# Cosformer attention and an MLP mixer on one core: the first batch in halves of the heads, its u inside the output's products

## Chip, core and metric

The kernel runs on one core of one Trainium2 chip. The metric is device time in microseconds of one execution. TensorE (PE in the profile) does the matrix products and writes PSUM; VectorE (DVE) and ScalarE (ACT) carry results from PSUM to SBUF; GpSimd (POOL) casts in SBUF; SyncE (SP) does nothing but issue transfers. Each engine works its own instructions in the order in which the program writes them, and waits for the others by semaphores. PSUM is handed out in two pools: `ps_mm` with four tiles of one bank, `ps_at` with two tiles of two banks.

## The reference

For each of 8 batches (8 heads, 576 positions, 64 values per head), attention without softmax and then an MLP over positions and one over channels:

```
phi(x) = concat(relu(x) * cos(theta_s), relu(x) * sin(theta_s))      # 64 -> 128 features
kv  = einsum(phi(k), v)            z = sum over s of phi(k)
x   = einsum(phi(q), kv) / (einsum(phi(q), z) + 1e-6)                # (576, 512), heads side by side
u   = x + (relu(x.T @ w_tok1) @ w_tok2).T                            # w_tok1 576x256, w_tok2 256x576
out = u + relu(u @ w_ch1) @ w_ch2                                    # w_ch1 512x1536, w_ch2 1536x512
```

Inputs and output are float32; the products run in bfloat16.

## The kernel before

**Tiles.** The 576 positions are four chunks of 128 (`R` = 4, position 4p + r in partition p of chunk r) and a tail of 64 (`R` again, as the index of the fifth chunk). The tails of two batches share one tile of 128 partitions, the even batch in the lower half, the odd one in the upper. `ORDER` = 0, 1, 2, tail, 3 is the order in which chunks are worked.

**Two halves of a batch.** `Front` is attention and token mixing: features of k and q (`feature`, line 276 on DVE and 274 on ACT), values into `v_aug` (287 on ACT, 289 on DVE or POOL), `kv` (334), q turned to have features in partitions (`q_trans`, 354, and `q_trans_last` for the tail, 366; copied to SBUF by ACT, 358 and 369), `num` (382, then the division on DVE, 390 to 392), `tok1` (405, relu in 410 and 412), `tok2` (429, sum with x on DVE in 432, giving u). `Channel` is the channel MLP: `c_main` (573) makes 12 blocks `mi` of w_ch1's product, each of four matmuls of 512 columns, whose relu ACT writes to `h1T` (577); `o_step` (606) adds two of 12 w_ch2 products to an output chunk; the last adds u (DVE, 611) and stores (615).

**Order.** All order is written out by hand (`manual_schedule`, line 76). The front of batch b + 1 is woven into the channel steps of batch b: `pieces` (483) lists (slot, piece), and the loop from line 784 runs step i and then the pieces of slot i. Batch 0 has nothing to hide behind: `first_front` (667) writes its front out instruction by instruction, with `busy` (210), matmuls on zeros into an unused PSUM tile, where TensorE would wait. It ends with u of batch 0 made directly in transposed form: `turned_x` (448) turns x through an identity product, `turned_b` (455) adds the token mixing, lines 743 and 744 copy to `uT`, and `c_block` (583) makes the first three blocks of the channel product, one quarter of the contraction at a time. Plain u, which the output needs, is made by `tok2` in slots 4 to 10 of batch 0's channel (plan from line 494).

**Batch 0's steps.** Steps 0 to 11 are the 12 blocks of c (the first three are done by then); steps 12 to 23 do output chunks 0 and 1 in thirds of w_ch2 (four products of chunk 0, four of chunk 1, and so on), steps 24 to 35 chunks 2 and 3. `O` = 12 in the plan. Batch 1's kv, turned q, num, tok1 and tok2 lie in slots 11 to 25.

**Loads.** SP issues, in this order: q of batch 0's first four heads, q's tail, k in two halves of the heads, k's tail, v's first half, its tail, v's second half, w_tok1, w_tok2, eight pieces of w_ch1, then batch 1's k, v and q, each with its tail (lines 104 to 137 and 750 to 769). The second half of q is issued by ACT. The weights land as float32 in tiles that are used for other things later. ACT casts w_tok1 (220) and permutes w_tok2 (223, 225); POOL casts w_ch1 (217). The tail rows of w_tok1 come by two casting transfers from POOL (200). w_ch2 comes in three casting transfers from POOL (204), written in slot 8 between POOL's two casts of batch 1's values (289). Batch 2's k and q wait for the second of these three (line 796).

Of the kernel before, what the change touches and what calls it, by code (L numbers as in the profile page):

```python
# [16 lines left out]
def kernel(  # L17
# [76 lines left out]

    def tiles():
        return tuple(io.tile([P, H, R * D], F32, name=n) for n in ("qt", "vt", "kt"))
# [19 lines left out]
    w_tok1n = stage1[:, 0:R * D_tok].rearrange("p (r t) -> p r t", r=R)  # L116
    w_tok2n = stage2[:, 0:NT * S].rearrange("p (n s) -> p n s", n=NT)
    nc.sync.dma_start(out=w_tok1n, in_=moe_w_tok1[0:SM, :].rearrange("(p r) t -> p r t", r=R))
    nc.sync.dma_start(out=w_tok2n, in_=moe_w_tok2.rearrange("(n t) s -> t n s", t=P))
# [77 lines left out]
    nc.gpsimd.memset(tail0.kp[half(1)], 0.0)  # L197
# [21 lines left out]
    def cast_tok1(mi):  # L219
        nc.scalar.copy(w_tok1[:, :, mi * P:(mi + 1) * P], w_tok1n[:, :, mi * P:(mi + 1) * P])  # L220

    def permute_tok2(ki):
        nc.scalar.copy(w_tok2[:, ki, 0:SM].rearrange("t (r p) -> t r p", r=R),
                       w_tok2n[:, ki, 0:SM].rearrange("t (p r) -> t r p", r=R))
        nc.scalar.copy(w_tok2[:, ki, SM:].rearrange("t (g s) -> t g s", g=2),
                       w_tok2n[:, ki, None, SM:S].to_broadcast([P, 2, ST]))


    class Front:
        def __init__(self, b, res, tail):  # L230
# [5 lines left out]

            self.alone = b < 2
            self.kp, self.qp, self.d_sb = {}, {}, {}

            self.qpT = once.tile([P, R * H, P], BF16, name="qpT")  # L240
            self.kv_sb = [twos.tile([P, HH, DP], BF16, name=f"kv_sb{g}") for g in range(2)]
            self.x = once.tile([P, R, Dm], BF16, name="x_sb")
# [16 lines left out]
        def feature(self, which, ci, j, heads=(0, H), on_act=False):  # L259
# [8 lines left out]
            else:  # L268
                t = self.tail
                dst, src = (t.kp, t.kt) if which == "k" else (t.qp, t.qt)  # L270
                rows = self.rows if self.alone else slice(0, P)
                w, o_ap, i_ap = w[rows], dst[rows, lo:hi, j, :], src[rows, lo:hi, :]
            if on_act:
                nc.scalar.activation(o_ap, i_ap, AF.Relu, bias=bias0[0:w.shape[0]], scale=w)
# [16 lines left out]
        def ksum(self, ci, heads=(0, H)):  # L291

            if not hasattr(self, "ks_ps"):
                self.ks_ps = ps_mm.tile([P, H], F32, name="ks_ps", tag="mm")
                self.ks_first = True
# [550 lines left out]
```

## Time and profile before

| what | value |
|---|---|
| median of 3 runs | 269.82 us (269.08 to 270.65) |
| the profiled execution | 270.21 us, span 268.4 us |
| batch 0's front until its first c block product (583) | 0 to 24.33 us |
| first three c blocks | 24.33 to 26.92 us |
| the other nine, and u of batch 0 | 26.92 to 36.87 us |
| batch 1's kv until the outputs take w_ch2's second third | 36.87 to 43.98 us |
| from there to batch 1's first c product | 43.98 to 57.51 us |
| the rest | 57.51 to 268.4 us |

The span is the stretch from the first to the last instruction that the profile shows. In a timeline each line gives start, duration from the first start to the last end, engine, source line, operation, destination and source tiles, shape and count, and in brackets the idle time of the engine before it and what ended that. In the chain of waits each line is a start, a length and what the end of the program hung on then. Weight tiles are named by the buffer they land in: `u_sb` is both w_tok1's and w_tok2's landing place, `w_stage`, `o_stage` and `u_stage` are w_ch1's.

### The profile page before, as it was taken

What the parts mean: (1) busy time and instruction counts of PE and PEld (TensorE: products, weight loads), DVE (VectorE), ACT (ScalarE), POOL (GpSimd) and SP (SyncE); (2) the same over time, 40 slices, a digit from 0 to 9 for tenths busy, and PEclk for the clock granted to TensorE, in tenths of its full rate; (3) what the DMA queues carried; (4) which work ended last, traced back from release to release, by engine and by line L of the source; (5) the groups of instructions that cost most, each with busy time, mean ns of one, the idle gap of its engine ahead of it and who ended that gap; (6) DMA issues with size and microseconds to landing.
All of it is one profiled execution on the core that took longest, in us unless ns stands there. A gap on an engine that the chain in (4) does not pass through costs nothing.

```text
span 268.4 us, 5119 instructions
## 1 busy us (share of the span) xinstructions
PE 259.9 (97%) x2026; PEld 138.9 (52%) x2047; DVE 164.3 (61%) x378; ACT 129.2 (48%) x230; POOL 15.5 (6%) x34
## 2 busy tenths in 40 slices
PE   7989999999999999999999999999999999999994
PEld 2665456455644455446644455446644455445543
DVE  4964598785566846776565846776565846820022
ACT  3955885328606372546606362546516362526400
POOL 5008150010000000000000000000000000000000
PEclk9999999999999999999999999999999999999999
DMA  7999999979999999389954989479974580280032
GB/s 216 316 383 395 327 169 197 330 176 280 196 333 293 265 204 324 114 212 271 228 207 117 286 188 322 120 187 235 242 248 117 156 120 0 59 199 0 2 114 81
DMA packets 92263, 55.25 MB, mean 206 GB/s; under 512 B 59472, under 2 KB 85968, under 8 KB 92240
## 3 DMA queue, kind: packets, MB, share of 16 engines
q1 hardware_dynamic: 89808, 52.24, 72.3%
q0 software_dynamic: 1904, 2.16, 4.5%
q10 hardware_dynamic: 528, 0.52, 0.6%
q8 instruction: 16, 0.26, 0.4%
q14 instruction: 7, 0.06, 0.1%
HBM read 35.85 MB, written 9.44 MB: 169 GB/s over the span
## 4 chain that ended last, share of the span: by engine, by line
PE 78%; DMA 11%; SPq 4%; DVE 4%; issue 1%; POOL 1%
PE o_ps L606 33%; PE c_ps L573 24%; PE u_ps L429 6%; PE b_ps L405 6%; PE ct_ps L593 4%; DMA w_stage<-in_moe_w_ch_dram 4%; DMA vt<-in_v_dram 4%; DMA w_ch<-in_moe_w_ch_dram 3%; PE kv_ps L334 3%; DVE x_sb L392 2%; PE num_ps L382 2%; SPq L86 2%; SPq L92 2%; DVE den L390 1%; DVE den L391 1%
## 5 line engine op out<-in xcount | busy, mean ns | idle before, releaser
L606 PE MATMUL o_ps<-w_ch,h1T 128*128 128x512 bf16 (+1 forms) x380 | 92.6, 372 | 0.9 <-DMA w_ch<-in_moe_w_ch_dram 0.2
L573 PE MATMUL c_ps<-uT,w_ch 128*128 128x512 bf16 (+2 forms) x384 | 91.9, 372 | 0.1
L577 ACT ACTIVATE h1T<-c_ps 128x512 bf16<-128x512 f32 x93 | 55.4, 598 | 59.5 <-PE c_ps L573 59.2
L606 PEld LDWEIGHTS <-h1T 128*128 128x128 bf16 x396 | 37.3, 98 | 40.1 <-issue 0.5
L573 PEld LDWEIGHTS <-w_ch 128*128 128x128 bf16 x384 | 33.5, 97 | 29.9 <-issue 0.2
L611 DVE TENSOR_TENSOR o_sb<-o_ps,u_sb 128x512 f32<-128x512 f32 (+1 forms) x33 | 22.2, 674 | 29.9 <-PE o_ps L606 29.8
L436 ACT CAST u_bf<-u_sb 128x512 bf16<-128x512 f32 x28 | 17.2, 618 | 16.8 <-DVE u_sb L432 13.3
L432 DVE TENSOR_TENSOR u_sb<-u_ps,x_sb 128x512 f32<-128x512 f32 x32 | 21.7, 688 | 5.7 <-PE u_ps L429 5.6
L429 PE MATMUL u_ps<-B,w_tok 128*128 128x512 bf16 x79 | 22.5, 379 | 0.2
L410 ACT ACTIVATE B<-b_ps 128x512 bf16<-128x512 f32 (+1 forms) x9 | 4.8, 549 | 33.7 <-PE b_ps L405 33.7
L392 DVE TENSOR_TENSOR x_sb<-num_ps,den 128x512 bf16<-128x512 f32 x28 | 19.4, 691 | 1.0
L593 PEld LDWEIGHTS <-w_ch 128*128 128x128 bf16 x192 | 13.9, 98 | 8.7
L276 DVE TENSOR_SCALAR kp<-kt,cos_t 128x512 bf16<-128x512 f32 x32 | 15.4, 485 | 4.7 <-DMA kt<-in_k_dram 4.7
L405 PE MATMUL b_ps<-x_sb,w_tok 128*128 128x512 bf16 x63 | 17.7, 379 | 0.1
L593 PE MATMUL ct_ps<-uT_tail,w_ch 128*128 128x128 bf16 x192 | 16.9, 219 | 0.0
L276 DVE TENSOR_SCALAR qp<-qt,cos_t 128x512 bf16<-128x512 f32 (+1 forms) x34 | 15.4, 453 | 1.4 <-DMA qt<-in_q_dram 1.3
L287 ACT CAST v_aug<-vt 128x512 bf16<-128x512 f32 (+1 forms) x28 | 15.6, 594 | 0.1
L276 DVE TENSOR_SCALAR qp<-qt,sin_t 128x512 bf16<-128x512 f32 (+1 forms) x34 | 15.4, 452 | 0.0
L611 DVE TENSOR_TENSOR o_sb<-o_ps,u_tail 128x512 f32<-128x512 f32 x4 | 2.8, 692 | 19.0 <-PE o_ps L606 19.0
L382 PEld LDWEIGHTS <-qpT 128*128 128x128 bf16 x256 | 11.5, 98 | 5.2 <-issue 0.8
L382 PE MATMUL num_ps<-kv_sb,qpT 128*128 128x65 bf16 x256 | 12.9, 193 | 0.5 <-DVE x_sb L392 0.5
L276 DVE TENSOR_SCALAR kp<-kt,sin_t 128x512 bf16<-128x512 f32 x28 | 13.4, 480 | 0.0
(96 smaller groups left out, 225.1 us busy)
## 6 DMA issues: line engine op xcount, KB each, us to landing
out_dram<-o_sb SPq DMA_DIRECT2D x29, 256.0 KB, 2.9
kt<-in_k_dram SPq DMA_DIRECT2D x7, 1024.0 KB, 6.7
vt<-in_v_dram SPq DMA_DIRECT2D x7, 1024.0 KB, 6.8
qt<-in_q_dram SPq DMA_DIRECT2D x7, 1024.0 KB, 8.8
w_stage<-in_moe_w_ch_dram SPq DMA_DIRECT2D x3, 512.0 KB, 10.3
w_ch<-in_moe_w_ch_dram POOLq DMA_DIRECT2D x3, 512.0 KB, 8.6
out_dram<-o_sb SPq DMA_DIRECT2D x10, 128.0 KB, 2.4
qtt<-in_q_dram SPq DMA_DIRECT2D x8, 128.0 KB, 5.5
```

Of the source, the lines that this page charges most:

```text
L276: nc.vector.tensor_scalar(o_ap, i_ap, scalar1=w, scalar2=0.0, op0=ALU.mult, op1=ALU.max)
L382: nc.tensor.matmul(num_ps[:, g, j * DP:j * DP + D1], self.qT_of(ci, h), self.kv_sb[g][:, j, 0:D1], start=True, stop=True)
L392: nc.vector.tensor_mul(self.x_of(ci)[rows].rearrange("p (g j d) -> p g j d", g=2, j=HH), nv[:, :, :, 0:D], den.to_broadcast([rows.stop - r ...
L405: nc.tensor.matmul(self.b1_ps[mi], w, self.x_of(ci), start=(ci == ORDER[0]), stop=(ci == ORDER[-1]))
L429: nc.tensor.matmul(u_ps, w_tok2[:, ki, ci * P:(ci + 1) * P], self.B1[:, ki, :], start=(ki == 0), stop=(ki == NT - 1))
L432: nc.vector.tensor_add(u, u_ps[rows], self.x_of(ci)[rows])
L436: nc.scalar.copy(self.ub[:, ci, :], u)
L573: nc.tensor.matmul(c_ps[:, lo:hi], w_ch1[:, ki, mi * P:(mi + 1) * P], uT[:, lo // P:hi // P, ki, :], start=(ki == 0), stop=(ki == NCC - 1))
L577: nc.scalar.activation(self.h1T[:, mi, :], c_ps, AF.Relu)
L593: nc.tensor.matmul(self.ct_ps[:, mi % R, :], w_ch1[:, ki, mi * P:(mi + 1) * P], self.tail.uT[:, ki, :], start=(mi % R == 0 and ki == 0), s ...
L606: nc.tensor.matmul(o_ps, h, w_ch2[:, ki, cols], start=ki == 0, stop=ki == NCH - 1)
L611: nc.vector.tensor_add(o_sb, o_ps, u)
```

## The change

Batch 0's front works in two halves of four heads each, from k's features to the turned products; token mixing gives half of B's columns per pass. Its kv, kept in `ps_mm`, its sums of k, denominators, products and divisions exist once per half. w_tok1's cast and one half of w_tok2's permutation go from ACT to POOL. The tail rows of w_tok1 come in float32 through SP. Blocks 0 to 2 of c begin when half of the turned blocks are there.

The tail queries of batches 0 and 1 are loaded into the unused half of the tile that takes their tail keys, so that one pair of feature instructions makes both (`load_beside`, `q_trans_beside`).

Batch 0 makes no plain u of its four chunks. `o_mix` starts each output's sum with w_tok2's product, and x is added instead of u at the end. x of batch 0 therefore lives until the outputs are stored, and batch 1's x takes a buffer of the `keep` pool; `B1` gets two buffers.

In the plan for batch 1, k's features, the values and kv come later, and kv, turned q and the first products are put together in slot 13, behind two `o_mix` steps, with four `busy` matmuls. Batch 0 has four more steps.

```diff
+    def load_beside(dst, src, b):
+        return nc.sync.dma_start(out=dst[half(1 - b)],
+                                 in_=src[b, :, SM:S, :].rearrange("h s d -> s h d"))
...
-    load_tail(qtt0, q, 0)
     load_main(kt0, k, 0, 0, HH)
-    load_main(kt0, k, 0, HH, H)
     load_tail(ktt0, k, 0)
+    load_beside(ktt0, q, 0)
     load_main(vt0, v, 0, 0, HH)
     load_tail(vtt0, v, 0)
+    load_main(kt0, k, 0, HH, H)
     load_main(vt0, v, 0, HH, H)
...
     nc.sync.dma_start(out=w_tok1n, in_=moe_w_tok1[0:SM, :].rearrange("(p r) t -> p r t", r=R))
+    for g in range(2):
+        nc.sync.dma_start(out=w_tail1n[half(g), :], in_=moe_w_tok1[SM:S, :])
...
-    for g in range(2):
-        nc.gpsimd.dma_start(out=w_tail1[half(g), :], in_=moe_w_tok1[SM:S, :])
...
+    def cast_tok1(ci):
+        if ci < R:
+            nc.gpsimd.tensor_copy(w_tok1[:, ci, :], w_tok1n[:, ci, :])
+        else:
+            nc.gpsimd.tensor_copy(w_tail1, w_tail1n)
+
+    def permute_tok2(ki, copy):
+        copy(w_tok2[:, ki, 0:SM].rearrange("t (r p) -> t r p", r=R),
+             w_tok2n[:, ki, 0:SM].rearrange("t (p r) -> t r p", r=R))
+        copy(w_tok2[:, ki, SM:].rearrange("t (g s) -> t g s", g=2),
+             w_tok2n[:, ki, None, SM:S].to_broadcast([P, 2, ST]))
...
+        def num_half(self, ci, g):
+            num_ps = ps_at.tile([P, 2, 512], F32, name="num_ps", tag="at")[:, 0, :]
+            for j in range(HH):
+                nc.tensor.matmul(num_ps[:, j * DP:j * DP + D], self.qT_of(ci, g * HH + j),
+                                 self.kv_sb[g][:, j, 0:D], start=True, stop=True)
...
+        def tok1_half(self, ci, g):
+            for mi in range(NT):
+                if ci == ORDER[0]:
+                    self.b1_ps[mi, g] = ps_mm.tile([P, DH], F32, name="b1_ps", tag="mm")
...
+                nc.tensor.matmul(self.b1_ps[mi, g], w, self.x_of(ci)[:, g * DH:(g + 1) * DH],
+                                 start=(ci == ORDER[0]), stop=(ci == ORDER[-1]))
...
+        def q_trans_beside(self):
...
+            qT_ps = ps_mm.tile([P, H, ST], BF16, name="qT_ps", tag="mm")
             for h in range(H):
                 nc.tensor.transpose(qT_ps[:, h, :],
...
+                                    self.tail.kp[rows, h, :, :].rearrange("p a b -> p (a b)"),
+                                    ident[rows, rows])
+            nc.scalar.copy(self.tail.qpT[:, :, half(g)], qT_ps)
...
+                plan = [(6, KS, 0), (6, KS, 1), (8, KS, 2, True), (9, KS, 3, True), (9, KS, R),
+                        (10, before.tok2, R, None, False), (11, V, 0, act), (11, V, 2, pool),
+                        (11, load_w_ch2, 0), (11, V, 3, pool), (11, load_w_ch2, 1),
+                        (11, load_w_ch2, 2), (11, V, R, nc.vector), (11, V, 1, act)]
+                plan += [(O + 1, KV, ci) for ci in range(NSC)]
+                plan += [(O + 1, self.kv_out, (0, 1), (0, 1)), (O + 1, self.q_trans_beside),
+                         (O + 1, QS, 0), (O + 1, fill, 2), (O + 1, QT, 0),
+                         (O + 1, QS, 1), (O + 1, fill, 1), (O + 1, QT, 1),
+                         (O + 1, QS, 2), (O + 1, fill, 1), (O + 1, QT, 2), (O + 1, N, R),
+                         (O + 1, QS, 3, True), (O + 1, N, 0), (O + 2, N, 1), (O + 3, QT, 3),
+                         (O + 5, N, 2), (O + 6, N, 3), (O + 8, before.tail_cast)]
...
-                at, mix, t = (), O + 7, O + 11
+                at, mix, t = (), O + 7, O + 9
...
-            plan += [(mix, self.mix_head, 0), (mix + 1, self.mix_head, 1),
-                     (mix + 2, self.mix_tail)]
...
+            plan += [(mix, self.mix_head, 0), (mix + 1 - first, self.mix_head, 1),
+                     (mix + 2 - first, self.mix_tail)]
...
+        def o_mix(self, ci):
+            self.o_ps[ci] = ps_mm.tile([P, Dm], F32, name="o_ps", tag="mm")
+            for ki in range(NT):
+                nc.tensor.matmul(self.o_ps[ci], w_tok2[:, ki, ci * P:(ci + 1) * P],
+                                 self.res["B1"][:, ki, :], start=(ki == 0), stop=False)
...
     def first_front(f):
...
         for ci in range(R):
...
+            f.feature("k", ci, 0, heads[0])
+            f.feature("k", ci, 1, heads[0])
+            busy(idle_ps, 2)
+            f.ksum(ci, 0)
+            f.values(ci, nc.scalar, heads[0])
         f.k_side(R)
...
+        f.q_trans_beside()
         for ci in range(R):
...
+            f.feature("k", ci, 0, heads[1])
+            if ci < 3:
+                f.feature("k", ci, 1, heads[1])
         for ci in range(NSC):
             f.kv(ci, (0,))
         f.kv_out((0,))
...
+        for ci in range(NSC):
+            cast_tok1(ci)
+        permute_tok2(1, nc.gpsimd.tensor_copy)
         cast_ch1()
...
+        f.kv_out((1,), on_act=(1,))
+        f.num_half(ORDER[4], 0)
+        f.dens(1)
+        f.dens_out(1)
+        permute_tok2(0, nc.scalar.copy)
+        for ci in ORDER[:2]:
+            f.num_half(ci, 1)
+        for ci in ORDER[2:]:
+            f.tok1_half(ci, 0)
+        for mi in range(NT):
+            f.tok1_out_half(mi, 0)
+        for kb in range(2):
+            t_ps[kb] = ps_mm.tile([P, SM], F32, name="t_ps", tag="mm")
+            f.turned_x(t_ps[kb], kb)
+        for i in range(3):
+            f.num_half(ORDER[i + 2], 1)
+            if i < 2:
+                f.tok1_half(ORDER[i], 1)
...
+        for kb in range(2):
+            turned(kb, nc.scalar.copy)
+        for ci in ORDER[2:]:
+            f.tok1_half(ci, 1)
+        for mi in range(NT):
+            f.tok1_out_half(mi, 1, on_act=(mi == 0))
...
+        for mi in range(2):
+            c.c_block(mi, 0)
+        for kb in (2, 3):
+            turned(kb, nc.vector.tensor_copy if kb == 3 else nc.scalar.copy)
...
-            if tails and (b % 2 == 0 or b == 1):
+            if tails and (b % 2 == 0 or b == 1 and n != "q"):
                 load_tail(tail_dst, src, b | 1)
+            if b == 1 and n == "k":
+                load_beside(ktt, q, b)
...
-            if b == 0 and i == NCH:
+            if b == 0 and i == NCH + 2:
                 load_batch(2, "kq", behind=w_ch2_done[1], tails=False)
```

`turned(kb, copy)` is `turned_b` and the copy to `uT`. `tok1_out_half` is the relu of one half on ACT or DVE.

More of the change, by code (lines that the diff above doesn't have):

```diff
@@ L332, in kv @@
+        def kv(self, ci, halves=(0, 1)):
+            if ci == 0 and halves == (0, 1):
+                both = ps_at.tile([P, 2, 512], F32, name="kv_ps", tag="at")
+                self.kv_ps = {g: both[:, g, :] for g in range(2)}
+            elif ci == 0:
+                self.kv_ps[halves[0]] = ps_mm.tile([P, 512], F32, name="kv_ps", tag="mm")
             for g in halves:
@@ L746, in first_front @@
+        for mi in range(2):
+            c.c_block(mi, 1)
+        for kb in range(2):
+            c.c_block(2, kb)
+        for kb in (2, 3):
             for mi in range(AHEAD):
```

259 lines of the change are left out of this document (115 added, 144 removed).

## Prediction

> **What bounds the kernel now.** I read the page first, then the stretches, then the chain of waits in order of time, then the timelines of ScalarE and SP. The page:
>
> ```profile
> span 268.4 us, 5119 instructions
> PE 259.9 (97%) x2026; PEld 138.9 (52%) x2047; DVE 164.3 (61%) x378; ACT 129.2 (48%) x230; POOL 15.5 (6%) x34
> ```
>
> TensorE is busy nearly throughout, so time is won only by fewer matmuls or by waits that end earlier. The stretches (us, then busy time and count of each engine, granted clock, DMA share, GB/s) show where waits are left:
>
> ```profile
> 24.33:26.92 2.59, 2.59 (x13) 1.18 (x12) 0.72 (x2) 0.54 (x2) 2.17 (x5) 1.00 1.08 382
> 26.92:36.87 9.95, 9.90 (x46) 4.50 (x46) 6.78 (x14) 8.30 (x16) 4.35 (x7) 1.00 1.00 279
> 36.87:43.98 7.11, 6.37 (x112) 4.76 (x112) 6.13 (x16) 5.70 (x9) 0.17 (x1) 1.00 1.12 174
> 43.98:57.51 13.53, 13.42 (x74) 6.35 (x76) 10.79 (x23) 5.10 (x8) 0.61 (x1) 1.00 0.84 254
> 57.51:268.40 210.89, 206.46 (x1523) 109.12 (x1535) 122.62 (x272) 93.75 (x166) 0.61 (x1) 1.00 0.73 185
> ```
>
> Behind 57.51, where batch 1's channel begins, nothing is changed and TensorE is full but for the last store; so I carry the start of that channel through to the end. Ahead of it there are two soft places: the head up to 24.33, and 36.87 to 43.98. The DMA share is about 1.0 through the first 44 us, and the chain says what that means:
>
> ```profile
> 11.27 10.33 DMA w_stage<-in_moe_w_ch_dram
> 21.62 1.85 SPq L92
> 23.52 9.93 DMA vt<-in_v_dram
> 33.50 0.62 POOL v_aug L289
> 34.12 0.73 POOL w_ch L204
> 34.84 0.54 POOL v_aug L289
> 35.39 8.55 DMA w_ch<-in_moe_w_ch_dram
> 44.41 0.59 PE o_ps L606 x2
> ```
>
> Up to 44 us the chain runs through transfers and not through the head: batch 1's v lands at 33.45, POOL casts it and only then issues w_ch2, whose second third lands at 35.39 + 8.55 = 43.94. The head could end earlier and this would stand. On ScalarE's timeline the head has a wait of its own:
>
> ```profile
> 19.29 1.10 ACT L223 CAST w_tok<-u_sb 128x512 bf16<-128x512 f32 x1 [1.86 <-DMA u_sb<-in_moe_w_tok_dram]
> ...
> 20.50 1.14 ACT L223 CAST w_tok<-u_sb 128x512 bf16<-128x512 f32 x1
> ...
> 22.03 0.66 ACT L410 ACTIVATE B<-b_ps 128x256 bf16<-128x256 f32 x2 [0.20 <-PE b_ps L405]
> ```
>
> w_tok2 lands at 19.28 (issued 10.28, 9.0 us), and ScalarE does nothing else until then.
>
> **Prices.** 512 columns: 4.32 us for 20 = 0.216; 256 columns half of it, 0.108. A 65-column product with its weights: 40 from 36.87 to 38.07 = 0.03. ScalarE by the distance of successive starts: 512 elements 0.50, a feature 0.73, a turned q of 1024 1.01, kv 0.36, a relu of a half 0.33. A division on DVE 0.62, a half of it 0.36, its two preparations 0.2 each.
>
> **The head.** What is removed: two tail features (0.47 each), the second pass over w_tok2 on ScalarE, two w_tok1 casts there (0.62 each). On DVE features of k's first half now end at 9.88 + 8 x 0.265 = 12.0, both tails at 12.8, the second half at 15.2. Its k lands later, being issued behind v's half and tail: in its place the tail of v now lands at 13.3, when DVE is ready at 13.2. Denominators, products and divisions of half 0 follow until about 18.1, token mixing of half 0 until 19.1, and TensorE has turned x's first two blocks by 19.5. Then it wants PSUM for half 1's token mixing. Of the four tiles, handed out in turn (row by row, c blocks without idle on TensorE show that it isn't the tile just used), the two next are those of half 0's B, and their relu stands on ScalarE **behind the permutation that waits for w_tok2**. So: 19.29 + 1.21 (to the next start in the rows above) = 20.50, two relus 0.33 each, 21.16. From there TensorE has half 1's token mixing, 9 x 0.108, two num of half the heads, 8 x 0.03, eight turned products 1.73, eight turnings at 0.056 (16 of them and two products of 0.216 from 21.28 to 22.61) 0.45, twelve c products 2.59: sum 6.0. Inside it I find no further wait: the copies to uT (0.59) and the second relus end 0.3 us or more ahead of their products. Fourth c block: **27.2**, before 26.92. A head without that wait would go on at 19.75 and give 25.9.
>
> At nothing I cost here: POOL's five casts and a permutation. They lie between w_tok1's landing (16.0) and the first w_ch1 piece (20.36), where POOL was idle; five at half of 0.61 end by 17.7, the permutation, 0.8 to 1.2, by 20.5. If that cover is gone, c block 4 is next: it needs casts that end at 25.2 and comes at 28.1. Ten more weight loads: 0 (inside 0.108 each) to 10 x 0.03; 0. The w_tail transfers: two issues on SP, 0.4 to 0.6 each, between w_tok1 and w_tok2, 64 KB each; they leave POOL's queue. SP is blocked there by landings, eight transfers back (u_stage is issued at 19.29, when w_tok2 lands), so w_tok2 may land between 0.7 earlier and 0.4 later; I take 19.3.
>
> **From 27.2 to w_ch2's second third.** Nine c blocks 7.78, tail u 0.43: 35.4. The four u of batch 0 are gone here (8 x 0.216 = 1.73), two `o_mix` come in (0.86): 36.3, where before kv began at 36.87. But values 0 and 1 now stand on ScalarE behind the relu of block 11: that ends at 36.0, they at 36.5 and 37.0, and kv ends at 38.0, before 38.07. **The gain of the shorter order is gone in this wait.** Then one chain on ScalarE: both kv copies (before one was DVE's) 38.9, tail q 39.4, turned q 0, 1, 2 at 40.4, 41.4, 42.4, the sine half of q's chunk 3 at 43.15. Turned q 3 on TensorE needs it and stands in slot 15, ahead of the rest of w_ch2's first third: 43.6; four output products and num 2 (0.86 + 0.22): **44.7** at the first product that takes w_ch2's second third, before 43.98.
>
> That third: batch 1's q tail now comes ahead of v on SP, so v lands later by its 128 KB: 0 (if it fits an idle moment) to 0.75 (qtt's issue at 1.26), 0.4 by 330 GB/s. POOL issues w_ch2 as much later: 43.95 + 0.4 = 44.35. It stays under 44.7, by a little. Batch 2's k, behind it on SP, moves with it: issued at 44.09 now, first used at 55.80, so 0. Four `busy` matmuls, 0.86, lie in the ScalarE chain: 0; with that gone, +0.86.
>
> **From there to batch 1's channel.** Before: 60 products of 512 x 0.216 = 12.96, two num 0.44, 13.4 (measured 13.53). Now two `o_mix` that were u work earlier are behind this point: 64 x 0.216 = 13.8, one num 0.22. And tok2 has one step (0.43) instead of two behind the last token mixing, whose relu on DVE takes 0.68: a wait of 0.25. 14.3. The transposes have 30 output products behind them instead of 20: 0. Four additions on DVE less, 4 x 0.69: 0, DVE waits there. The buffers that live longer (x, B) cost 0: batch 2's x is written some ten us behind batch 0's last output; if not, TensorE would wait there for what is missing.
>
> **Sum:** 44.7 + 14.3 = 59.0 against 57.51: +1.5, span 269.9. The profiled execution (268.4 + 1.8 around it = 270.2) is 0.4 above the median of 269.82; against the median 271.3. A difference below 0.5%, 1.35 us, can hardly be told from none.
>
> **Rivals.** (1) *The head is won, the transfer sets the time.* w_tok2 lands early enough, 25.9; then kv waits for POOL's second cast (35.9), ends at 36.5, ScalarE's chain ends at 42.3, TensorE stands at 43.8 and waits for w_ch2 at 44.35: + 14.2 = 58.5, **270.8**. For it: 1.3 us hang on one landing. Against: the rows give 19.29.
> (2) *Not slower: w_ch2 comes sooner.* DVE's features beside POOL's work at 33.5 to 36 took 0.68 to 0.73 instead of 0.48; now DVE is emptier then. If POOL's issues shorten and the third lands at 43.0, and ScalarE's chain ends by 42, the channel begins at 43.0 + 14.05 = 57.05, **269.4**. It decides from 43.45 (57.5 - 14.05) at the first product; a gain of over 0.5% needs 42.1. For it: the third's transfer took 8.55 us, the next one hardly longer. Against: it starts with v's landing, which the change delays. The Trainium skill, GPSIMD Engine Reference, section 1 Specifications, says that GpSimd shares its SBUF interfaces with VectorE in some modes; the 0.48 to 0.73 agrees, and by it the third would come up to 0.5 us sooner.
> (3) *More waits in the head.* If PSUM comes back in another order, so that turned x waits too (+0.6), or TensorE stops for its instructions as at 19.63 (0.63, "issue"): both, with ScalarE's chain behind them, 1.5 + 1.2 = +2.7, **272.5**.
> (4) *The clock.* The 12 first fills took 5.30 us, 0.44 each, against 0.216 later. If 1.1 us of waiting at 19.75 brings that rate back for as long, 12 x 0.22 = 2.7 more than the sum: **274.0**. Against: after the waits of 0.54 and 0.63 at 18.04 and 19.63 products held 0.216. The Trainium skill, TensorE: Matmul & The Clock Gate, Part 1, puts the return to half rate at an idle window of about 3.4 us; by that it would not happen here.
>
> **Chances.** Forecast 0.52 (its own range 270.6 to 272.2; of it 0.38 is over 271.17, slower, 0.14 within 0.5%); (1) 0.12 (0.10 within, 0.02 slower); (2) 0.18 (0.08 within, 0.10 faster, below 268.47); (3) 0.14 and (4) 0.04, slower. Faster 0.10, same 0.32, slower 0.58. The range leaves out 0.1 at each end: 269.0, inside (2), to 272.8, which holds (3).
>
> **What would show it.** ScalarE's permutation starting when w_tok2 lands, with TensorE idle until the two relus behind it; the fourth c block at 27.2; values 0 and 1 on ScalarE behind block 11's relu; TensorE waiting in slot 15 for q's chunk 3; the first product with the second third at 44.7, not waiting for its DMA; batch 1's channel at 59.0. It is wrong if that channel begins before 57.5, or if TensorE has no idle between 19.5 and 21.

## The result and the profile after

The changed kernel takes **271.19 us** (five runs, 271.06 to 271.65) beside 269.86 us for the kernel before (five runs, 269.08 to 270.65): ratio 1.0051, 95% interval [1.0027, 1.0074]. It is slower by about the bound that the prediction gave for a difference that can be told from none. The profiled execution took 271.65 us, again some 0.45 above its median. Its page:

```profile
span 269.8 us, 5150 instructions
PE 261.2 (97%) x2041; PEld 140.5 (52%) x2062; DVE 159.9 (59%) x379; ACT 127.6 (47%) x231; POOL 16.6 (6%) x38
```

Its stretches (us, then busy time and count of PE, PEld, DVE, ACT and POOL, granted clock, DMA share, GB/s), cut at the same events as before: the fourth c block, k'v, the first product with w_ch2's second third, batch 1's channel:

```profile
25.89:35.44 9.55, 9.17 (x42) 4.11 (x42) 4.62 (x10) 8.39 (x16) 3.63 (x7) 1.00 0.95 282
35.44:43.91 8.47, 7.28 (x122) 5.48 (x124) 5.91 (x16) 6.07 (x9) 0.51 (x1) 1.00 1.16 178
43.91:58.37 14.46, 14.37 (x78) 6.42 (x76) 9.86 (x20) 4.28 (x8) 0.61 (x1) 1.00 0.73 227
58.37:269.80 211.43, 206.55 (x1523) 109.17 (x1535) 122.57 (x272) 93.72 (x166) 0.61 (x1) 1.00 0.75 184
```

Set against the prediction, term by term (us of the span):

| stretch | before | after | predicted |
|---|---|---|---|
| up to the fourth c block | 26.92 | 25.89 | 27.2 |
| on to the first product with w_ch2's second third | 17.06 | 18.02 | 17.5 |
| on to batch 1's channel | 13.53 | 14.46 | 14.3 |
| the rest | 210.89 | 211.43 | 210.9 |
| span | 268.4 | 269.8 | 269.9 |

The sum came out, and two of its terms did not: the head is 1.0 us faster, not 0.3 slower, and the rest, which was to stay as it was, is 0.5 longer. The head first, by a row of GpSimd and three of ScalarE:

```profile
16.24 1.20 POOL L232 CAST w_tok<-u_sb 128x512 bf16<-128x512 f32 x1
...
17.73 1.11 ACT L232 CAST w_tok<-u_sb 128x512 bf16<-128x512 f32 x1
18.73 0.30 ACT L234 CAST w_tok<-u_sb 128x128 bf16<-128x128 f32 x1
19.20 0.66 ACT L359 ACTIVATE B<-b_ps 128x256 bf16<-128x256 f32 x2 [0.17 <-PE b_ps L353]
```

The permutation (L232, one half on each engine) waits for no DMA, so w_tok2 had landed by 16.24; before, it began at 19.29 after 1.86 us of waiting. So the two relus of half 0 (L359) are ready for TensorE at once, and the row names TensorE as what they waited for.

In the middle the chain of waits (start, us, what; in order of time) no longer runs through transfers:

```profile
33.22 1.04 PE c_ps L609 x4
34.29 0.60 ACT h1T L613
34.88 1.03 ACT v_aug L301 x2
35.96 1.13 PE kv_ps L371 x32
...
38.45 1.02 ACT qpT L395
39.51 0.61 PE qT_ps L391 x8
40.84 0.71 DVE x_tail L426
41.68 0.41 PE num_ps L419 x8
```

Relu of block 11 (L613), values 0 and 1 (L301), k'v, a copy of turned queries (L395), a division on VectorE (L426): TensorE goes from one to the next and waits for ScalarE or VectorE between them. The waits themselves, in brackets on TensorE's timeline:

```profile
35.44 1.41 PE L371 MATMUL kv_ps<-v_aug,kp 128*128 128x65 bf16 x32 [0.33 <-ACT v_aug L301]
...
39.51 0.61 PE L391 MATMUL qT_ps<-ident,qp 128*128 128x128 bf16 x8 [0.22 <-ACT qpT L395]
...
41.68 0.41 PE L419 MATMUL num_ps<-kv_sb,qpT 128*128 128x65 bf16 x8 [0.64 <-DVE x_tail L426]
42.14 0.38 PE L649 MATMUL o_ps<-w_ch,h1T 128*128 128x512 bf16 x1
42.36 0.61 PE L391 MATMUL qT_ps<-ident,qp 128*128 128x128 bf16 x8
```

Between 35.44 and 43.91 TensorE has 1.19 us of idle (8.47 - 7.28). Before, 36.87 to 43.98 had 0.74 (7.11 - 6.37). Among what it works there and did not before are the four idle products, 0.86 by their price.

### The profile page after: what moved, and what is told of

Same layout as the page of the kernel before. It is cut to its first block, busy times and chain, and to the rows that moved or that the text cites. A ratio compares the mean times of both kernels' runs of the same rounds, so it can differ in the third digit from the quotient of the medians.

```text
span 269.8 us, 5150 instructions
## 1 busy us (share of the span) xinstructions
PE 261.2 (97%) x2041; PEld 140.5 (52%) x2062; DVE 159.9 (59%) x379; ACT 127.6 (47%) x231; POOL 16.6 (6%) x38
## 4 chain that ended last, share of the span: by engine, by line
PE 88%; DVE 5%; DMA 3%; issue 1%; ACT 1%; SPq 0%; POOL 0%; POOLq 0%; DVEq 0%
PE o_ps L649 33%; PE c_ps L609 25%; PE u_ps L460 6%; PE b_ps L436 6%; PE idle_ps L218 4%; PE ct_ps L629 3%; PE kv_ps L371 3%; DVE x_sb L426 2%; PE num_ps L419 2%; DMA qtt<-in_q_dram 2%; PE qT_ps L391 1%; DMA qpT_tail<-qp_tail 1%; PE c_ps L619 1%; PE b_ps L353 1%; DVE den L424 1%
## 5 line engine op out<-in xcount | busy, mean ns | idle before, releaser
L613 ACT ACTIVATE h1T<-c_ps 128x512 bf16<-128x512 f32 x93 | 55.4, 598 | 61.3 <-PE c_ps L609 61.0
L609 PEld LDWEIGHTS <-w_ch 128*128 128x128 bf16 x384 | 33.5, 97 | 29.8
L658 DVE TENSOR_TENSOR o_sb<-o_ps,u_sb 128x512 f32<-128x512 f32 (+1 forms) x29 | 19.5, 672 | 27.3 <-PE o_ps L649 25.3
L460 PE MATMUL u_ps<-B,w_tok 128*128 128x512 bf16 x71 | 20.2, 379 | 0.2
L441 ACT ACTIVATE B<-b_ps 128x512 bf16<-128x512 f32 x7 | 4.2, 597 | 33.2 <-PE b_ps L436 33.2
L463 DVE TENSOR_TENSOR u_sb<-u_ps,x_sb 128x512 f32<-128x512 f32 x24 | 16.5, 690 | 5.6 <-PE u_ps L460 5.6
L290 DVE TENSOR_SCALAR kp<-kt,cos_t 128x512 bf16<-128x512 f32 (+1 forms) x36 | 16.1, 450 | 3.9 <-DMA kt<-in_k_dram 3.9
L426 DVE TENSOR_TENSOR x_sb<-num_ps,den 128x512 bf16<-128x512 f32 x24 | 16.6, 691 | 0.8
L301 ACT CAST v_aug<-vt 128x512 bf16<-128x512 f32 (+1 forms) x31 | 16.6, 576 | 0.1
L290 DVE TENSOR_SCALAR kp<-kt,sin_t 128x512 bf16<-128x512 f32 (+1 forms) x33 | 14.9, 452 | 0.0
L218 PE MATMUL idle_ps<-zeros,ident 128*128 128x512 bf16 x33 | 12.0, 469 | 1.6 <-POOL ident masks.py:199 1.4
L436 PE MATMUL b_ps<-x_sb,w_tok 128*128 128x512 bf16 x48 | 13.3, 379 | 0.0
L419 PEld LDWEIGHTS <-qpT 128*128 128x128 bf16 x224 | 10.1, 98 | 5.5 <-ACT qpT L395 1.5
```

What stands on the lines that cost most here:

```text
L218: nc.tensor.matmul(dst, ident, zeros[:, 0:dst.shape[-1]], start=True, stop=True)
L290: nc.vector.tensor_scalar(o_ap, i_ap, scalar1=w, scalar2=0.0, op0=ALU.mult, op1=ALU.max)
L301: nc.scalar.copy(dst, src)
L426: nc.vector.tensor_mul(self.x_of(ci)[rows].rearrange("p (g j d) -> p g j d", g=2, j=HH), nv[:, :, :, 0:D], den.to_broadcast([rows.stop - r ...
L436: nc.tensor.matmul(self.b1_ps[mi], w, self.x_of(ci), start=(ci == ORDER[0]), stop=(ci == ORDER[-1]))
L460: nc.tensor.matmul(u_ps, w_tok2[:, ki, ci * P:(ci + 1) * P], self.B1[:, ki, :], start=(ki == 0), stop=(ki == NT - 1))
```

## The experiments

Three questions were open: which part of the change costs, what inside that part, and what became of the 1.0 us of the head. Each run is set against the kernel before as it was measured beside it: its medians were 270.12 for the first four runs, 269.73, 269.77 and 269.67 for the three later groups. "Stretch" below is the time from the fourth c block (512 columns) to batch 1's channel, each from one trace: 30.59 in that of before, 32.48 in that of after (18.02 + 14.46).

### Head alone, plan alone, two edits of the loads

**Head alone**: the changed kernel with the old plan, and u of batch 0 as a step of its own again.

```diff
-                plan = [(6, KS, 0), (6, KS, 1), (8, KS, 2, True), (9, KS, 3, True), (9, KS, R),
...
+                plan = [(4, KS, 0), (4, u, 0, ps_at, False), (5, u, 1, ps_at, False),
+                        (5, KS, 1), (5, KS, 2, True), (6, u, 2, None, False), (6, KS, 3, True),
...
-                for ci in (0, 1):
-                    steps.append(lambda ci=ci: self.o_mix(ci))
```

> The new head and loads with the old plan: u of batch 0 by tok2, kv in slot 11, no fills, no o_mix. If the changed kernel's loss sits in the plan behind the head, the fourth c block comes at 25.9 (as in the changed kernel), the first product with w_ch2's second third at 43.2 (0.75 earlier than before), batch 1's channel at 56.6 to 56.8, and the time is 0.7 to 0.9 below before: 269.0. If the head's gain is lost again in the old plan too, because the transfers set the time, the channel begins at 57.4 and the time is 269.8.

Measured: 269.84, ratio 0.9988 [0.9973, 1.0003]. The head is as in the changed kernel (fourth c block at 25.85), but batch 1's channel begins at 57.28, only 0.23 sooner than before. TensorE's timeline shows where the rest went:

```profile
38.16 0.62 PE L388 MATMUL qT_ps<-ident,qp 128*128 128x128 bf16 x8 [0.55 <-DVE qp L287]
39.96 0.39 PE L640 MATMUL o_ps<-w_ch,h1T 128*128 128x512 bf16 x1 [1.17 <-DMA w_ch<-in_moe_w_ch_dram]
```

It waited 1.17 us for w_ch2's first third. The gain of the head met a transfer.

**Plan alone**: the kernel before, its head and loads untouched, with the new plan and `o_mix`.

```diff
-                plan = [(4, KS, 0), (4, u, 0, ps_at, False), (5, u, 1, ps_at, False),
...
+                plan = [(6, KS, 0), (6, KS, 1), (8, KS, 2, True), (9, KS, 3, True), (9, KS, R),
...
+        def o_mix(self, ci):
+            self.o_ps[ci] = ps_mm.tile([P, Dm], F32, name="o_ps", tag="mm")
```

> The old head and loads with the new plan and u summed within the output's products. If the plan is what loses, it costs about 2.0 us on the old head as well: batch 1's channel at 59.4 to 59.7, time 271.9. If the plan only suits the new head's times and loses nothing by itself, the channel begins at 57.5 to 58.0 and the time is 270.0.

Measured: 273.01, ratio 1.0112 [1.0097, 1.0127]. The stretch runs from 27.12 to 59.61: 32.49, as in the changed kernel (32.48) to 0.01, though all that lies ahead of it is 1.2 later. So **the length of the new plan is its own**, whenever it begins. This run says something of the loads too. They are those of the kernel before, yet on ScalarE the permutation of w_tok2 starts with no wait:

```profile
17.10 1.10 ACT L223 CAST w_tok<-u_sb 128x512 bf16<-128x512 f32 x1
```

So w_tok2 had landed by 17.1 here and at 19.28 in the profiled execution of before: between two executions with the same loads, each of its own kernel, the landing moved by 2 us. TensorE did not come sooner for it: the fourth c block is at 27.12 here and at 26.92 there. The first cast of v starts at 32.23 here, at 33.50 in before's profile, at 32.45 in the changed kernel.

**Tail rows of w_tok1 through SP, in float32**, in the kernel before:

```diff
-    for g in range(2):
-        nc.gpsimd.dma_start(out=w_tail1[half(g), :], in_=moe_w_tok1[SM:S, :])
+    for g in range(2):
+        nc.sync.dma_start(out=w_tail1n[half(g), :], in_=moe_w_tok1[SM:S, :])
...
+        nc.gpsimd.tensor_copy(w_tail1, w_tail1n)
```

> Before with one thing changed: the tail rows of w_tok1 come in float32 through SP and POOL casts them. If the casting transfers from POOL are what held the first loads up, w_tok2 lands at 16.5 to 17.5 instead of 19.28 and batch 1's v about 1 us earlier than 33.45, time 269.2. If the order of SP's loads did it, w_tok2 stays at 19 and the time at 269.9.

Measured: 270.05, ratio 1.0018 [0.9996, 1.004]: no effect that can be told. In its trace w_tok2 has landed by 17.23 and POOL's first cast of v starts at 32.25, as the first theory has it; but the plan alone shows 17.10 and 32.23 with the old transfers, so the edit is not what brought this.

**Order of SP's first loads alone**, in the kernel before (k's second half behind v's first half and tail):

```diff
-    load_tail(qtt0, q, 0)
     load_main(kt0, k, 0, 0, HH)
-    load_main(kt0, k, 0, HH, H)
     load_tail(ktt0, k, 0)
+    load_tail(qtt0, q, 0)
     load_main(vt0, v, 0, 0, HH)
     load_tail(vtt0, v, 0)
+    load_main(kt0, k, 0, HH, H)
```

> Before with one thing changed: SP's first loads in the new order (k's first half, both 64-row tails, v's first half and tail, k's second half). If this order is what brings the loads in earlier, q's first half lands at 5.4 instead of 6.1, w_tok2 at 16.5 to 17.5 and v of batch 1 about 1 us earlier; k's second half comes later, at 13, and DVE waits for it up to 2 us, so the time is 269.5 to 271. If the casting transfers did it, w_tok2 stays at 19.

Measured: 272.03, ratio 1.0083 [1.0067, 1.01]. Without work in halves of the heads the later k delays the head: fourth c block at 28.91. By itself the order only costs. (Which part of the new head wins its 1.0 us, beside the loads, was not tried further.) And since everything had landed by then, this run gives the old plan's length with no transfer in its way: 28.91 to 58.48, **29.57**. The new plan is 2.9 longer than that (32.48 and 32.49 against 29.57).

### What inside the plan

Four edits of the changed kernel. The first takes the idle products out, the second gives ScalarE's last key feature to VectorE, the third puts num R ahead of turned q 2, the fourth is all three:

```diff
-                         (O + 1, QS, 0), (O + 1, fill, 2), (O + 1, QT, 0),
+                         (O + 1, QS, 0), (O + 1, QT, 0),
...
-                plan = [(6, KS, 0), (6, KS, 1), (8, KS, 2, True), (9, KS, 3, True), (9, KS, R),
+                plan = [(6, KS, 0), (6, KS, 1), (8, KS, 2, True), (9, KS, 3), (9, KS, R),
...
-                         (O + 1, QS, 2), (O + 1, fill, 1), (O + 1, QT, 2), (O + 1, N, R),
+                         (O + 1, QS, 2), (O + 1, fill, 1), (O + 1, N, R), (O + 1, QT, 2),
```

No idle products:

> The changed kernel without the four idle products (two, one, one) between the turned products of batch 1's queries. Theory 'covered': TensorE gets past them only to wait for ScalarE, whose three copies of turned queries run end to end from 38.45; without the four, the first turned product is ready 0.4 sooner, but ScalarE is busy with the copy of the last queries until 38.27, so the copies start 0.18 sooner and everything behind by as much: 271.0, ratio to the kernel before 1.0045. Rival 'each costs its 0.216': 4 x 0.216 = 0.86 sooner, 270.3, ratio 1.002; the product with w_ch2's second third would then begin at 43.05, which is where that third lands (43.2), so 270.4 at best.

Key chunk 3 on VectorE:

> The changed kernel with both halves of key chunk 3 on VectorE, which is idle from 31.73 to 33.42 there; ScalarE loses one 0.81 us sine half in front of block 11's relu and of values 0 and 1. Theory 'the full ScalarE queue is what the new plan pays for': values 0 and 1 end 0.8 sooner, k'v begins at 34.95 where the products before it end and runs at 1.23 instead of 1.58, the copies begin at 37.6 instead of 38.45; the product with the second third begins at 43.1 to 43.2: -0.7, 270.5, ratio 1.0025. Rival 'the queries set it': q lands at 35.45 and VectorE's six halves end at 38.17 in either case, so the third turned product cannot begin before 38.2 and the wait for the division of the last tokens stays: -0.2, 271.0, ratio 1.0045.

Last tokens first:

> The changed kernel with the product of the last tokens (num R) ahead of the turned product of query chunk 2 instead of behind it. Theory 'num 1 waits for VectorE's division of the last tokens (40.40 to 41.53), because of two PSUM tiles': the division starts at 39.4, num 1 is issued at 40.9 instead of 41.68. What comes next is the sine half of query chunk 3 on ScalarE, which ends at 42.01 behind the three copies: turned product 3 then waits until 42.0 instead of beginning at 42.36: -0.35, 270.8, ratio 1.0035. Rival 'each stall is worth what it shows': -0.64 to -0.8, 270.4, ratio 1.002. Rival 'nothing': the copies of turned queries on ScalarE set the end and the wait moves there: 271.2, ratio 1.005.

All three:

> The three edits together (no idle products, key chunk 3 on VectorE, last tokens' product first). Theory 'transfer gate': the product with w_ch2's second third cannot begin before that third lands, about 43.2, whatever is freed ahead of it, and 14.5 us of products stand behind it (13.5 in the plan before, whose u is summed earlier): batch 1's channel at 57.7, 270.5, ratio 1.0025, the same as the best of the three alone. Rival 'the stalls add up' (0.2 + 0.7 + 0.35 or more): 1.3 to 1.9 sooner, 269.3 to 269.9, ratio 0.998 to 1.0, with the product with the second third at 42.3 or before.

| kernel | time | ratio to before | stretch |
|---|---|---|---|
| changed | 271.19 | 1.0051 [1.0027, 1.0074] | 32.48 |
| no idle products | 271.10 | 1.0058 [1.0042, 1.0074] | 32.21 |
| key chunk 3 on VectorE | 271.25 | 1.0059 [1.0044, 1.0073] | 32.55 |
| last tokens first | 270.82 | 1.0044 [1.003, 1.0057] | 32.09 |
| all three | 270.81 | 1.0041 [1.0026, 1.0056] | 31.81 |

The intervals of the five overlap, so what follows is read from the stretches. The idle products are mostly covered: 0.27 of their 0.86. Key chunk 3 on VectorE brought nothing, and its ScalarE rows, with k'v from TensorE's timeline, say why:

```profile
33.98 0.60 ACT L613 ACTIVATE h1T<-c_ps 128x512 bf16<-128x512 f32 x1 [0.70 <-PE c_ps L609]
34.47 1.13 ACT L301 CAST v_aug<-vt 128x512 bf16<-128x512 f32 x2
...
35.13 1.41 PE L371 MATMUL kv_ps<-v_aug,kp 128*128 128x65 bf16 x32 [0.33 <-ACT v_aug L301]
```

ScalarE now has time to spare and waits 0.70 itself, for block 11's products. Values 0 and 1 stand behind that relu and cannot use the time: the wait at k'v is 0.33 as before. So the wait goes with their place in the queue and not with the queue's load.

Last tokens first did in the trace as its theory said. Num 1 is issued at 40.82 instead of 41.68, and the next wait is the one for the sine half of query chunk 3:

```profile
42.02 0.62 PE L391 MATMUL qT_ps<-ident,qp 128*128 128x128 bf16 x8 [0.37 <-ACT qp L288]
```

All three together give 0.67 of the stretch. The second third had landed by 43.30, when SP issues the load behind it, and its first product ran at 43.50, so the gate left little more. Even together the waits that these edits remove are worth under a quarter of the new plan's 2.9 us; for each that goes, the next stands right behind.

### What became of the head's gain

In the run with the head alone, the first third of w_ch2 was issued at 33.14, behind the first cast of v. What the transfers did then, by stretches (columns as above; the last two are DMA share and GB/s):

```profile
31.00:33.50 2.50, 2.50 (x13) 1.17 (x12) 2.50 (x6) 1.80 (x4) 1.05 (x2) 1.00 1.05 354
33.50:36.00 2.50, 2.50 (x20) 1.20 (x19) 2.44 (x4) 2.50 (x6) 2.50 (x4) 1.00 0.48 65
36.00:38.50 2.50, 1.95 (x53) 1.78 (x49) 2.45 (x6) 2.50 (x5) 0.08 (x1) 1.00 1.23 202
```

The transfer engines, busy at about 1.0 through the first 44 us by the coarse stretches, move 65 GB/s from 33.5 to 36.0: batch 1's q is through, and w_ch2 has been issued but has hardly begun. So its issue might come sooner at no one's cost. One edit tries it: the first third hangs on a relu of batch 0's channel instead of on v.

```diff
+    relus = []
     def load_w_ch2(third):
...
+        if third == 0:
+            after(w_ch2_done[0], relus[-1])
...
-                        (8, load_w_ch2, 0), (8, V, 3, pool), (8, load_w_ch2, 1),
+                        (6, load_w_ch2, 0), (8, V, 2, pool),
+                        (8, V, 3, pool), (8, load_w_ch2, 1),
...
-                nc.scalar.activation(self.h1T[:, mi, :], c_ps, AF.Relu)
+                relus.append(nc.scalar.activation(self.h1T[:, mi, :], c_ps, AF.Relu))
```

It was made in three kernels. In the one with the new head and the old plan:

> The head and loads of the changed kernel with the plan of the kernel before, and w_ch2's first third issued on GpSimd behind the relu of c block 6 (about 30.8) instead of behind the first cast of v (33.14). Theory 'the head's gain of 1.0 is real and was lost to w_ch2': in the run without this, TensorE waited 1.17 at 38.79 to 39.96 for that third. The third's data then begin about 33 instead of 35.9, it lands near 38, and nothing waits for it; the plan's own length from the fourth c block to batch 1's channel is 29.6 where no transfer is in its way (the run with the late head): 25.85 + 29.6 + 0.5 for query chunk 1 = 55.9 to 56.0 instead of 57.28: 268.4, ratio 0.995. Rival 'the transfers are full': the third's packets take their time from q and v of batch 1, whose casts and features come later by as much; 269.8, ratio 0.999.

In the kernel before:

> The kernel before with the same one edit (w_ch2's first third behind the relu of c block 6, about 31.8, instead of 34.06). Theory 'w_ch2 sets the kernel before as well': its waits for w_ch2 (0.16 to 0.43 by the traces) and the late second third go; fourth c block at 26.8, and 29.6 to 30.1 behind it: 56.4 to 56.9 instead of 57.51: 269.2, ratio 0.9975. Rival 'TensorE was only 0.2 from its own limit': 269.7, ratio 1.0.

In the changed kernel (behind block 7's relu, at slot 7):

> The changed kernel with the same one edit (w_ch2's first third behind the relu of c block 7, about 30.8, instead of 33.00). Theory 'its own plan sets its time': the trace shows no wait for w_ch2, its waits are for ScalarE and VectorE and 14.5 us of products stand behind the second third's landing; nothing changes: 271.1, ratio 1.005. Rival 'the landing of the second third (43.2) is what the product at 43.91 waits for': up to 0.7 to 1.5 sooner, 269.9 to 270.4, ratio 1.001. Rival 'q comes later': the features of the queries begin later than 35.45: 271.7, ratio 1.007.

| kernel | time | ratio to before | fourth c block | channel | stretch |
|---|---|---|---|---|---|
| new head, old plan, w_ch2 sooner | 268.96 | 0.9957 [0.9934, 0.9979] | 26.10 | 55.82 | 29.72 |
| before, w_ch2 sooner | 269.82 | 0.9998 [0.9981, 1.0014] | 26.86 | 56.77 | 29.91 |
| changed, w_ch2 sooner | 271.93 | 1.0073 [1.0048, 1.0098] | 26.18 | 58.67 | 32.49 |

The first is faster than both kernels (without the edit it had 0.9988 [0.9973, 1.0003]; the two intervals overlap by 0.0006), and of its transfers the stretch from 33.5 to 36.0 shows the difference; the product that waited 1.17 now runs 1.46 sooner without a wait:

```profile
33.50:36.00 2.50, 2.50 (x13) 1.12 (x12) 2.44 (x5) 2.50 (x6) 1.94 (x3) 1.00 1.19 215
...
38.50 0.59 PE L643 MATMUL o_ps<-w_ch,h1T 128*128 128x512 bf16 x2
```

The changed kernel gets nothing from the same edit: its stretch is 32.49 once more. It was not waiting for w_ch2. The first and the third of these kernels have the same head and issue the third at 31.52 and 31.61; they differ in the plan, and by 2.97 us in time (271.93 - 268.96): so the plan's 2.9 us stand in the whole time too. In the kernel before, the channel begins 0.74 sooner than in before's profile, and the time is the same. Those 0.74 are not shown to be the edit's: with the tail rows through SP and w_ch2 as it was, the channel begins at 56.66. Where they went is in the section on the prediction, under the rest.

### The sum within the products, with the items spread

The last run keeps the sum of u within the output's products and takes the packing away:

```diff
-                plan += [(O + 1, KV, ci) for ci in range(NSC)]
-                plan += [(O + 1, self.kv_out, (0, 1), (0, 1)), (O + 1, self.q_trans_beside),
...
+                plan += [(11, KV, ci) for ci in range(NSC)]
+                plan += [(11, self.kv_out, (0, 1), (0, 1)), (11, QS, 0), (11, QS, 1),
+                         (O, QT, 0, (0, H), act, ps_at), (O, QS, 2), (O + 1, QT, 1),
+                         (O + 1, QT, 2), (O + 1, QS, 3), (O + 1, N, 0),
+                         (O + 2, self.q_trans_beside), (O + 2, N, 1),
+                         (O + 4, N, 2), (O + 4, QT, 3), (O + 6, N, R), (O + 8, N, 3),
...
-                at, mix, t = (), O + 7, O + 9
+                at, mix, t = (), O + 8, O + 12
```

> The changed kernel with w_ch2's first third issued behind the relu of c block 7, and with batch 1's items spread as the plan before had them: k'v right behind block 11, the turned products and numerators of the queries one or two to a step between the first products of the output, no idle products, values 0 and 1 in front of relus 10 and 11, all query features on VectorE. u is still summed within the output's products. It stands between the run with the new head, the old plan and the early third (fourth c block to batch 1's channel 29.7, ratio 0.9957) and the changed kernel with the early third (32.5, 1.0073). Theory 'the packing costs, not the summing': with products between the items the stretch is 29.7 to 30.3, since the four products of chunks 0 and 1 of the sum cover the wait for the queries' landing (35.4) and for w_ch2's first third (38.5): 269.0 to 269.6, ratio 0.996 to 0.998. Rival 'the summing costs': eight products that ran ahead of k'v now wait behind it, where the landing of q and of w_ch2 holds TensorE anyway, and nothing fills the place they left: 0.9 to 1.7 more, 30.6 to 31.4, 269.9 to 270.7, ratio 0.9995 to 1.0025. Rival 'neither': the wait is in what both share, 32 and more, 271.3, ratio 1.005.

Measured: 274.60 to 276.32 in four executions and 278.79 in the profiled one; the ratio by those four is 1.0219 [1.0193, 1.0246], outside every range that was given. TensorE's timeline and SP's queue:

```profile
53.86 2.75 PE L644 MATMUL o_ps<-w_ch,h1T 128*128 128x512 bf16 x12
64.57 4.53 PE L604 MATMUL c_ps<-uT,w_ch 128*128 128x384 bf16 x24 [7.95 <-DMA uT<-u_bf]
```

```profile
48.90 0.38 SPq L86 DMA_DIRECT2D vt<-in_v_dram  x1
49.33 1.47 SPq L92 DMA_DIRECT2D vtt<-in_v_dram  x2
50.84 5.12 SPq L92 DMA_DIRECT2D ktt<-in_k_dram  x2
56.06 0.97 SPq L657 DMA_DIRECT2D out_dram<-o_sb  x1
57.12 3.72 SPq L494 DMA_TRANSPOSE uT<-u_bf  x2
```

The edit put batch 1's u three slots later (t from O + 9 to O + 12) and its transposes two (O + 11 to O + 13), and the loads of batch 2's v and tails, which stay at step NCH + 12, now come ahead of u's transposes on SP. The transposes are issued at 57.12, where the changed kernel has them at 52.50, and TensorE waits 7.95 us for them, though ScalarE's last copy of the four chunks of u ends at 52.21. Up to 56.45 the granted clock of the profiled execution is 1.00. So the time of this kernel says nothing of the sum. Its products do: they end at 53.86 + 12 x 0.216 = 56.45, 30.29 behind the fourth c block at 26.16, with TensorE's wait for transposes not yet begun. In the changed kernel with the early third the same products take 32.49. **Some 2.2 of the 2.9 us go with the packing**, and some 0.7 (30.29 against 29.57) are left for the sum within the products. The packing means all that this edit takes back together: the items in one slot, the four idle products among them (0.27 by the run without them), values 0 and 1 behind relu 11, and the sine half of query chunk 3 on ScalarE. Which of these has how much was not tried. That a kernel with the sum and the spread items, and the loads put right, would reach the time that this gives was not tried.

## Why the prediction was right in sum and wrong in parts

**The head: wrong.** The step that failed: "SP is blocked there by landings [...] I take 19.3" for w_tok2. The row of 19.29 was right for that execution and not for the kernel: in the two other kernels with the loads of before ahead of it (the plan alone; before with the early third) the permutation starts at 17.10 and 16.98 without a wait, and with two more issues ahead of w_tok2 (tail rows through SP) at 17.23, having waited 0.32. With no late landing the permutation delays no relu, and the fourth c block came at 25.89: the 25.9 that the text gives for a head without that wait, as in rival 1. TensorE was busy for 1.45 of the 1.50 us between 19.5 and 21, the sign by which the text itself said it would be wrong. ScalarE's wait of 1.86 us stood in the trace of before, but TensorE did not pay for it even there: the fourth c block came at 26.92 with it, at 27.12 and 26.86 in the two kernels without it, and the row at 22.03 that the prediction shows names TensorE as what the relus behind the permutation waited for. What was to be asked is whether the wait belongs to the order of the queues or to the one execution. What a landing as late as 19.28 would have cost the new head stays open, since no execution of it shows one.

**The landing of v: too late by the same cause.** It was predicted 0.4 later. POOL's first cast of v starts at 32.45 in the changed kernel, 32.23 in the plan alone with the old loads: 0.2 later. The absolute 33.45 was the late execution again.

**Values 0 and 1 behind relu 11: right**, and borne out by the run with key chunk 3 on VectorE. It is 0.33 of wait and a slower k'v: 35.44 to 37.02, 1.58, where the run with the head alone, whose values stand earlier, has 35.78 to 37.00, 1.22.

**ScalarE's chain up to query chunk 3: right as a limit, wrong as the wait that is seen.** The text has turned q 3 wait for the sine half. In the changed kernel num 1 waits first, for VectorE's division of the last tokens, with two PSUM tiles between them; that was overlooked. With it out of the way the sine half is the wait (42.02 and 41.93 in the two runs). Size: 17.5 was predicted from the fourth c block to the second third, 18.02 measured.

**The idle products at 0: nearly right** (0.27 of stretch, nothing that can be told in the time). **From the second third on: right**, 14.3 against 14.46; the wait of 0.25 ahead of u is there, 0.20 us from 48.14 to 48.34.

**The rest: wrong.** "Behind 57.51 [...] nothing is changed [...] so I carry the start of that channel through to the end." From batch 2's channel on this holds: 27.50, 32.74, 27.50, 32.75, 27.50 from channel to channel, to 0.1 in all thirteen traces ahead of the last run's but for one place (27.78, before with the early third). But batch 1's channel took 33.05 in before and 33.65 in after, and 33.05 to 33.78 over the thirteen. The difference is one wait on TensorE's timeline, at 75.55 in the changed kernel:

```profile
75.55 0.42 PE L419 MATMUL num_ps<-kv_sb,qpT_tail 128*128 128x65 bf16 x8 [0.52 <-DMA qpT_tail<-qp_tail]
```

num R of batch 2 waits for the transpose of the last queries, which is the last of five on SP. The wait is none in before's profile, 0.62 and 0.33 in two kernels with before's plan (tail rows through SP; w_ch2 sooner). These two kernels had their channel 0.85 and 0.74 sooner than before's profile and gave 0.71 and 0.42 of it back in batch 1's channel; the second lost another 0.28 at the one place named above. The length of the wait goes with the time that SP takes to issue the three transposes of turned queries ahead of it: where that was 4.7 us or less, the wait was 0 to 0.34 (seven traces, 4.23 in before), where it was 5.4 or more, 0.52 to 0.65 (four, 5.41 in after), and at 4.85 it was 0.20 and 0.62. What makes them slow to issue was not tried. Two variants of the new plan (key chunk 3 on VectorE, last tokens first) have no wait there, so it is not the plan's own.

**The rivals.** (1) had the head right, but not its price: nothing waited for POOL's second cast or for w_ch2. (2) had its two conditions nearly met and still not its time: the second third had landed by 43.20, when SP issues the load behind it, and ScalarE's sine half ended at 42.01, but TensorE came to the product at 43.91, behind num 1's wait, turned q 3, four products and num 2. Made to come sooner still, w_ch2 gave the changed kernel nothing. Nor did POOL's work shorten: from its first cast of v to the end of its last issue of w_ch2 it took 3.50 us (32.45 to 35.95), before 3.54. (3) was not seen. (4), the clock: waits of 0.2 to 0.64 us left it at 1.00 in every stretch shown above, as did the one of 1.17 in the run with the head alone (1.00 from 38.5 to 41.0), and the wait of 7.95 in the last run did not, by its stretches:

```profile
56.45:64.57 8.12, 0.17 (x2) 0.01 (x1) 6.90 (x17) 0.00 (x0) 0.61 (x1) 0.80 1.11 184
64.57:68.93 4.36, 4.36 (x25) 2.44 (x25) 0.00 (x0) 0.19 (x1) 0.00 (x0) 0.59 1.04 226
69.60:72.00 2.40, 2.40 (x15) 1.10 (x13) 0.00 (x0) 1.79 (x4) 0.00 (x0) 1.00 0.42 94
```

The granted clock falls within the wait, from 1.00 ahead of 61.0 to 0.50 behind 62.0, over 4 us after the last product. It is 0.59 over the 24 products behind the wait, which take 4.36 instead of the 2.62 that they take without it: 0.50 until 68.0, 1.00 again from 68.5, nearly 4 us after they began. The Trainium skill, TensorE: Matmul & The Clock Gate, Part 1, has half rate after an idle window of about 3.4 us and full rate after as long a busy one; the trace agrees, with neither change sooner than that.

So the 0.1 us between the predicted span and the measured one is luck and no measure of the reasons: 1.3 too much in the head, 0.5 and 0.2 too little in the two middle terms, 0.5 too little in the rest, and these cancel.

## What to carry to other kernels

A landing time read from one execution is a sample: before a forecast hangs on it, ask what it would be if the transfer came 2 us sooner, and whether anything but that row makes it late. A faster stage is worth what the next gate lets through: here the head's 1.0 us brought the next channel 0.2 us forward until w_ch2 was issued 1.6 us sooner, and the engines' busy share over that stretch hid that they stood half idle just where it mattered. Waits packed into one place, with no products between them, are not paid off one at a time: each that was removed showed the next, while the same items, spread between products and without the idle ones, took 2.2 us less up to the same point.

## What the runs showed of the hardware

- A transfer that casts, issued by GpSimd, starts late and moves half: issued at 33.14 (0.89 us long) with the plain loads through, it left the engines at a share of 0.48 and 65 GB/s from 33.5 to 36.0; from there to 38.5 they gave 202 GB/s at a share of 1.23, where plain loads gave 354 at 1.05 from 31.0 to 33.5. That a cast from float32 reads two bytes for each that it writes would account for it, but was not measured by itself.
- The same loads landed up to 2 us apart in executions of kernels that are alike up to there: w_tok2 at 19.28 in before, by 16.98 in before with the early third. The profiled execution of before was still only 0.4 us from its median.
- A moved step moves its place in every queue that it uses: two slots put the transposes of u behind 8 us of issues on SP, for 7.95 us of waiting and another 1.7 us at the lower clock (4.36 - 2.62).
